# The last 64 contraction rows of a Q projection as pairs of 64-row tiles in front of the transpositions, with the order of all steps and the PSUM banks in a table

## The chip, the cores and the metric

The kernel runs on one core of one Trainium2 chip. The metric is the device time of one execution in microseconds. A core has five engines that work side by side: PE (matmuls, on an array of 128 by 128), DVE and ACT (elementwise work and reductions), POOL, and SP, which here issues most DMAs. Each engine runs its own list of instructions in order and waits on semaphores for the others. PE's results go to PSUM, which has 8 banks of 512 f32 values per partition; DVE and ACT bring them to SBUF.

## The reference

Two independent attention problems, A and B, of the same size, whose outputs are put side by side. Each projects x to queries, attends with 32 query heads over 16 cached key and value heads, and projects the result:

```python
B, Sq, D = 16, 80, 576
Hq, Hkv, Sk, Dh = 32, 16, 512, 128
q = (x @ wq).reshape(B, Sq, Hq, Dh).transpose(0, 2, 1, 3)
k = jnp.repeat(k_cache, 2, axis=1)
v = jnp.repeat(v_cache, 2, axis=1)
scores = jnp.einsum("bhqd,bhkd->bhqk", q, k) * Dh ** -0.5
p = softmax(scores, axis=-1)
o = jnp.einsum("bhqk,bhkd->bhqd", p, v)
out = o.transpose(0, 2, 1, 3).reshape(B, Sq, Hq * Dh) @ wo
```

All inputs are bf16. The Q projection contracts over D = 576 = 4 x 128 + 64 rows.

## The kernel before

**Units.** The work is cut into 128 units, numbered U: one batch entry and four key/value heads, so eight query heads of 80 rows each. Eight units (eight batch entries) of the same heads form an octet, `goct`; there are 16 octets, 8 per problem.

**Steps of a unit.** Scores stand with the query rows on the partitions. The two query heads of one key head have 160 rows: 128 of them form one whole-array matmul of 512 columns (`qk`, L686, four per unit), and the last 32 rows of all four key heads form one more score tile from four matmuls of 32 columns of the array (`qkr`, L672). For each of the five score tiles DVE takes the maximum (`max`, L695), ACT the exponential with its row sum (`exp`, L699), DVE the reciprocal of the sums (`rcp`, L705) and POOL the normalised rows (`nrm`, L708). Then 40 transpositions, `tr` (L741), bring the probabilities to key rows on the partitions. They are issued in 20 pairs: one half of a pair uses array rows 0 to 63, the other rows 64 to 127 (`tile_position=(64 * h, 0)`), and the two write different PSUM banks. Three copies (`ptev`, L758 on ACT, L760 on DVE) bring them to `pT`. The `pv` matmuls (L778: four groups per unit, four matmuls of 160 columns each) multiply with V; ACT copies two groups at a time into `oT` (`oev`, L794).

**Q projection.** For each octet, `em_qp` (L568) computes `qT` for the eight heads in two parts of the octet's 640 rows, 480 and 160 columns. Every part is five matmuls of 128 rows that add up in one bank. The fifth holds the 64 rows left over: `xT[:, half, 4]` holds the last 128 columns of x transposed, so its first 64 rows repeat rows that chunk 3 has, and the first 64 rows of `wq_sb[:, :, 4]` are zero (`em_wqz`, L400). ACT or DVE scales and stores the result (`qev`, L579 and L580).

**Output projection.** `op` (L828) multiplies 16 heads of `oT` by `wo` in tiles of 128 rows and 288 columns. The first half of the heads is copied to `acc` (L841, L843); the second is added to it (L859) and stored.

**Loads.** SP issues K as a transposing DMA (L640, five slots `kT`), V (L644, four slots), the weights, x and the stores. A K load waits until the last `qk` of the unit five earlier has read its slot. Problem A's x is transposed on PE (L492), problem B's by two DMAs per half (`em_ldxt` L509, `em_ldxt4` L513).

**Order.** Every step is added to `_Sched` with a key, resources that it reads and writes, and estimates of its duration. `arrange` plans with these: at each point it takes for the engine that is free first the ready step with the lowest priority value, picks one of the PSUM banks that the step's class may use (`BANKS`), and, on PE, groups steps of the same tile shape (`mode`: 0 whole array, 1 for `qkr`, 2 for `tr`). `finalize` derives the semaphore waits from the order that comes out, and each engine issues its own steps in that order. `LA` = 10 is how many score tiles the scores run ahead, `QL0`, `QL1` and `QL2` how many units ahead Q is done. One semaphore more, `e_tr`, makes the transposition group wait in its own middle.

Of the kernel before, what the change touches and what calls it, by code (L numbers as in the profile page):

```python
# [6 lines left out]
BF16 = mybir.dt.bfloat16  # L7
# [6 lines left out]
LA = 10  # L14
# [5 lines left out]
NS = 16  # L20
QL0 = 14.0
QL1 = 10.0
KC = 2.95
VK = 8.0
KK = 8.0
DLAT = 1.6
XC = 0.4
QL2 = 10.0
VC = 1.65
WQC = 3.2  # L30
NQ = 3
# [6 lines left out]
BANKS = dict(S=(0, 1, 2), T=(3, 4, 6), Y=(4, 6, 5), O=(5, 7, 4), M=(7, 5, 6, 3, 4), M0=(7, 5, 6, 3, 4), M1=(7, 6, 5), ML=(7, 5, 6, 0, 1))  # L38
NML = 12
XDMA = True  # L40
RG = ((0, 1, 2), (3, 4))
TS0 = 4.5
TSAME = 0.3
TNEXT = 0.05
# [5 lines left out]
PTO = -2.0  # L50
PTE = (('dve',), ('dve',), ('act', 'dve'))
QEV = ('act', 'dve')
OEO = 3.0
OVO = 2
QEO = 0.0
RCO = 3
NSS = 6
OPSPLIT = 2
XLD = ((-100.0, -60.0), (-25.0, -24.9))
XH = -2.0  # L60
WQ1 = -16.8
OPX = ((12.0, 1.8), (18.5, 1.45), (18.5, 1.45), (18.5, 1.45))
LP0 = 19
LPS = 1.05
LPC = 29.0
WOL = 1.2
WOA = (99.0, 99.0, 99.0, 99.0)
WOS = 1.0

MM0 = 0.0025  # L70
MM1 = 1.0 / 2400.0


def _mm(n, cols):
    return n * (cols * MM1 + MM0)


class _VB:
    __slots__ = ("cls", "phys", "left", "id")

    def __init__(self, cls, i):
        self.cls = cls
        self.phys = None
        self.left = 0
        self.id = i


class _Op:
    __slots__ = ("engs", "eng", "key", "seq", "emit", "reads", "writes", "dsem", "stream", "dur", "lat", "cost",
                 "alloc", "pri", "after", "pre", "start", "done", "mode",  # L90
# [3 lines left out]
class _Sched:  # L94

    def __init__(self):
        self.ops = []
        self.marks = {}
        self.nvb = 0

    def bank(self, cls):
        self.nvb += 1
        return _VB(cls, self.nvb)

    def add(self, eng, key, emit, reads=(), writes=(), dsem=None, name="", stream=None, dur=0.1, lat=0.15,
            cost=0.0, alloc=(), mode=0, ahead=0.0, after=None):
        op = _Op()
        op.engs = (eng,) if isinstance(eng, str) else tuple(eng)
        op.eng = op.engs[0]
        op.key = float(key)  # L110
        op.pri = op.key - ahead
        op.after = after
# [7 lines left out]
        op.dur = dur  # L120
        op.lat = lat
        op.cost = cost
        op.alloc = list(alloc)
        op.mode = mode
        op.deps = []
        op.pre = []
        op.start = op.done = None
        op.signals = False
        op.sidx = None
        op.waits = []  # L130
        op.clock = None
        self.ops.append(op)
        return op

    def arrange(self):
        ops = sorted(self.ops, key=lambda o: (o.key, o.seq))
        last_w, readers = {}, {}
        for op in ops:
            deps = {}
            for r, ver in op.reads:  # L140
                if isinstance(r, _VB):
                    r.left += 1
                w = last_w.get(r)
                assert w is not None, ("read of never-written resource", r, op.name)
                deps[id(w)] = w
            for r, ver in op.writes:
                w = last_w.get(r)
                if w is not None:
                    deps[id(w)] = w
                for rd in readers.get(r, ()):  # L150
                    deps[id(rd)] = rd
            deps.pop(id(op), None)
            for r, ver in op.reads:
                readers.setdefault(r, []).append(op)
            for r, ver in op.writes:
                last_w[r] = op
                readers[r] = []
            op.pre = list(deps.values())
        streams = {}
        for op in ops:  # L160
            streams.setdefault(op.stream, []).append(op)
        by_eng = {}
        for name, l in streams.items():
            assert all(o.engs == l[0].engs for o in l), name
            for e in l[0].engs:
                by_eng.setdefault(e, []).append(name)
        at = dict((name, 0) for name in streams)
        free = dict((e, 0.9) for e in by_eng)
        mode = 0
        bank_free = dict((b, 0.0) for b in range(8))  # L170
        dma_free = 1.4
        left = len(ops)
        hold = dict(pe=0.05, dve=0.02, act=0.02, pool=0.0, sp=0.0)

        def pick(vbs, now, used=()):
            if not vbs:
                return []
            c = sorted((max(bank_free[b], now), n_, b) for n_, b in enumerate(BANKS[vbs[0].cls])
                       if bank_free[b] is not None and b not in used)
            for t, n_, b in c:  # L180
                r = pick(vbs[1:], now, used + (b,))
                if r is not None:
                    return [(t, b)] + r
            return None

        def ready(o, now):
            t = 0.0
            if o.after is not None:
                d = self.marks[o.after]
                if d.start is None:  # L190
                    return None
                t = d.start
            for d in o.pre:
                if d.done is None:
                    return None
                if not (d.eng == "pe" and o.engs[0] == "pe"):
                    t = max(t, d.done)
            if o.alloc:
                c = pick(o.alloc, max(t, now))
                if c is None:  # L200
                    return None
                t = max([t] + [bank_free[b] for _, b in c])
            return t

        while left:
            best = None
            for e in free:
                cand = []
                for n in by_eng[e]:
                    if at[n] < len(streams[n]):  # L210
                        o = streams[n][at[n]]
                        r = ready(o, free[e])
                        if r is not None:
                            cand.append((r, o))
                if cand:
                    st = max(free[e], min(c[0] for c in cand))
                    if best is None or st < best[0]:
                        best = (st, e, cand)
            assert best is not None, [(streams[n][at[n]].name, [d.name for d in streams[n][at[n]].pre if d.done is None],
                                       len(streams[n][at[n]].alloc)) for n in streams if at[n] < len(streams[n])]  # L220
            now, e, cand = best
            if e == "pe":
                near = [c for c in cand if mode and c[1].mode and c[0] <= now + (TSAME if c[1].mode == mode else TNEXT)]
                cand = [c for c in near if c[1].mode == mode] or near or cand
                now = max(now, min(c[0] for c in cand))
            k_, s_, r, o = min(((o.pri, o.seq, r, o) for r, o in cand if r <= now + hold[e]), key=lambda x: x[:2])
            st = max(now, r)
            o.eng = e
            dur = o.dur[e] if isinstance(o.dur, dict) else o.dur
            if e == "pe":  # L230
                if o.mode and mode == 0 or o.mode != mode:
                    st = max(st, now + 0.1)
                mode = o.mode
            if o.alloc:
                for vb, (_, b) in zip(o.alloc, pick(o.alloc, max(r, now))):
                    vb.phys = b
                    bank_free[b] = None
            o.start = st
            free[e] = st + dur
            if o.dsem is not None:  # L240
                d0 = max(st + 0.5, dma_free)
                dma_free = d0 + o.cost
                o.done = dma_free + DLAT
            else:
                o.done = st + dur + o.lat
            for res, ver in o.reads:
                if isinstance(res, _VB):
                    res.left -= 1
                    if res.left == 0:
                        bank_free[res.phys] = o.done  # L250
            at[o.stream] += 1
            left -= 1
        self.end = max(o.done for o in ops)
        for n_, op in enumerate(sorted(ops, key=lambda o: (o.start, o.seq))):
            op.key = float(n_)
# [72 lines left out]
def bass_concat_heads__gqa_block_cached__gqa_block_cached__near_ridge_kernel(  # L328
# [27 lines left out]
    with ExitStack() as es:  # L356
# [42 lines left out]
        def em_wqz(e):  # L399
            return e.memset(wq_sb[0:64, :, 4, :], 0.0)  # L400
# [544 lines left out]
```

## Time and profile before

| | us |
|---|---|
| median of 3 runs | 739.16 (739.05 to 739.34) |
| the profiled execution | 739.38 |
| its span in the profile | 737.6 |
| PE, DVE, ACT, POOL busy in it | 730.7, 650.3, 625.7, 433.8 |
| granted TensorE clock, mean | 1.0 |

The largest PE groups by busy time are L568 (Q projection, 1280 matmuls, 206.0 us), L778 (PV, 2048, 189.4), L686 (scores, 512, 185.7), L828 (output projection, 1280, 180.5), L741 (transpositions, 5120, 96.9) and L672 (remainder scores, 512, 39.6).

How to read it: a group's busy time and mean duration come from records whose ends are modelled for PE, and matmuls are pipelined, so a matmul's record (233 ns for 160 columns) is longer than the distance from its start to the next matmul's start. Sums of PE's work are made from these distances. "us to landing" of a DMA is from its issue to the semaphore. Idle time is given with what released it.

### The profile page before, as it was taken

What the parts mean: (1) busy time and instruction counts of PE and PEld (TensorE: products, weight loads), DVE (VectorE), ACT (ScalarE), POOL (GpSimd) and SP (SyncE); (2) the same over time, 40 slices, a digit from 0 to 9 for tenths busy, and PEclk for the clock granted to TensorE, in tenths of its full rate; (3) what the DMA queues carried; (4) which work ended last, traced back from release to release, by engine and by line L of the source; (5) the groups of instructions that cost most, each with busy time, mean ns of one, the idle gap of its engine ahead of it and who ended that gap; (6) DMA issues with size and microseconds to landing.
All of it is one profiled execution on the core that took longest, in us unless ns stands there. A gap on an engine that the chain in (4) does not pass through costs nothing.

```text
span 737.6 us, 26159 instructions
## 1 busy us (share of the span) xinstructions
PE 730.7 (99%) x10818; PEld 510.8 (69%) x10818; DVE 650.3 (88%) x1344; ACT 625.7 (85%) x1827; POOL 433.8 (59%) x647
## 2 busy tenths in 40 slices
PE   9999999999999999999999999999999999999998
PEld 5566677677667676677677677666777677667776
DVE  4989999998999999888999999998889888998983
ACT  1889999999989889878889888989899888898881
POOL 1465666665666576556666565575565565665660
DMA  9999999999999999999999889999988978999920
GB/s 263 217 281 229 262 227 252 227 223 211 200 224 213 210 237 268 228 239 226 213 234 228 196 185 275 261 273 228 198 188 192 203 169 173 295 235 217 198 94 29
DMA packets 362102, 160.85 MB, mean 218 GB/s; under 512 B 276096, under 2 KB 358528, under 8 KB 361984
## 3 DMA queue, kind: packets, MB, share of 16 engines
q1 hardware_dynamic: 360768, 158.00, 97.3%
q8 instruction: 85, 1.39, 0.8%
q10 hardware_dynamic: 1216, 1.18, 0.5%
q14 instruction: 33, 0.27, 0.1%
HBM read 87.46 MB, written 2.95 MB: 123 GB/s over the span
## 4 chain that ended last, share of the span: by engine, by line
PE 96%; DVE 2%; ACT 1%; ACTq 0%; issue 0%
PE ps L568 23%; PE ps L828 21%; PE ps L778 19%; PE ps L686 15%; PE ps L741 12%; PE ps L672 5%; DVE negmax L695 1%; ACT p_sb L699 1%; PE ps L492 0%; DVE qT L580 0%; PE ps L429 0%; ACTq L545 0%; ACT oT L794 0%; ACT L448 0%; DVE pT L760 0%
## 5 line engine op out<-in xcount | busy, mean ns | idle before, releaser
L708 POOL TENSOR_SCALAR p_sb<-p_sb,rinv 128x512 bf16<-128x512 bf16 x640 | 431.4, 692 | 285.4 <-DVE rinv L705 283.5
L699 ACT ACTIVATE p_sb<-ps,negmax 128x512 bf16<-128x512 f32 x640 | 443.1, 701 | 27.8 <-DVE negmax L695 24.2
L695 DVE TENSOR_REDUCE negmax<-ps 128x1 f32<-128x512 f32 x640 | 416.2, 679 | 32.6 <-PE ps L672 16.8
L568 PE MATMUL ps<-xT,wq_sb 128*128 128x160 bf16 (+1 forms) x1280 | 206.0, 300 | 1.0 <-DVE xT L496 0.6
L778 PE MATMUL ps<-pT,v_sb 128*128 128x160 bf16 x2048 | 189.4, 233 | 0.0
L686 PE MATMUL ps<-kT,qT 128*128 128x512 bf16 x512 | 185.7, 380 | 0.0
L828 PE MATMUL ps<-wo_sb,oT 128*128 128x288 bf16 x1280 | 180.5, 286 | 0.0
L778 PEld LDWEIGHTS ps<-pT,v_sb 128*128 128x128 bf16 x2048 | 155.0, 98 | 35.1 <-DVE pT L760 0.6
L760 DVE COPY pT<-ps 128x1024 bf16<-128x1024 bf16 (+1 forms) x260 | 172.1, 676 | 6.0 <-PE ps L741 5.1
L568 PEld LDWEIGHTS ps<-xT,wq_sb 128*128 128x128 bf16 x1280 | 106.5, 98 | 66.1 <-issue 1.7
L828 PEld LDWEIGHTS ps<-wo_sb,oT 128*128 128x128 bf16 x1280 | 122.5, 98 | 40.6 <-issue 2.1
L699 ACT ACTIVATION_READ_ACCUMULATOR p_sb<-ps,negmax 128x1 f32 x640 | 137.5, 215 | 0.0
L794 ACT CAST oT<-ps 128x320 bf16<-128x320 f32 x256 | 108.7, 430 | 15.0 <-PE ps L778 14.1
L741 PEld LDWEIGHTS ps<-ident,p_sb 64*128 64x128 bf16 x5120 | 81.8, 95 | 37.9 <-issue 9.9
L741 PE MATMUL ps<-ident,p_sb 64*128 64x64 bf16 x5120 | 96.9, 190 | 0.0
L580 DVE TENSOR_SCALAR qT<-ps 128x480 bf16<-128x480 f32 (+1 forms) x131 | 65.2, 500 | 15.6 <-PE ps L568 14.7
L758 ACT COPY pT<-ps 128x256 f32<-128x256 f32 x124 | 47.3, 381 | 36.0 <-PE ps L741 35.4
L579 ACT ACTIVATE qT<-ps 128x160 bf16<-128x160 f32 (+1 forms) x125 | 52.8, 443 | 15.0 <-PE ps L568 14.3
L686 PEld LDWEIGHTS ps<-kT,qT 128*128 128x128 bf16 x512 | 49.6, 98 | 21.7 <-ACT p_sb L699 2.4
L705 DVE RECIPROCAL rinv<-rowsum 128x3 f32<-128x3 f32 (+1 forms) x256 | 41.2, 161 | 8.2 <-ACT p_sb L699 7.8
L672 PE MATMUL ps<-kT,qT 128*32 128x512 bf16 x512 | 39.6, 384 | 1.6 <-ACT p_sb L699 1.6
L859 DVE TENSOR_TENSOR osb<-ps,acc 128x288 bf16<-128x288 f32 x40 | 18.0, 451 | 16.1 <-PE ps L828 15.5
(25 smaller groups left out, 48.6 us busy)
## 6 DMA issues: line engine op xcount, KB each, us to landing
v_sb<-in_A_v_cache_dram SPq DMA_DIRECT2D x64, 512.0 KB, 4.8
v_sb<-in_B_v_cache_dram SPq DMA_DIRECT2D x64, 512.0 KB, 4.6
wo_sb<-in_A_wo_dram SPq DMA_DIRECT2D x8, 576.0 KB, 6.9
wo_sb<-in_B_wo_dram SPq DMA_DIRECT2D x8, 576.0 KB, 6.2
wq_sb<-in_B_wq_dram SPq DMA_DIRECT2D x4, 1024.0 KB, 7.1
out_dram<-osb SPq DMA_DIRECT2D x40, 72.0 KB, 3.7
wq_sb<-in_A_wq_dram SPq DMA_DIRECT2D x2, 1024.0 KB, 6.7
wq_sb<-in_A_wq_dram ACTq DMA_DIRECT2D x2, 512.0 KB, 6.9
```

The lines of the kernel that those rows point to most:

```text
L568: last = e.matmul(ps[:, vb.phys, 0:n1 - n0], lhsT=wq_sb[:, wsl, ck, i * 128:(i + 1) * 128], rhs=xT[:, half, ck, n0:n1], start=(ck == 0), s ...
L580: return e.tensor_scalar(dst, src, SCALE, None, op0=AluOpType.mult)
L672: last = e.matmul(ps[32 * g4:32 * g4 + 32, vb_.phys, :], lhsT=qT[:, qsl_, bl_, g4 * 160 + 128:g4 * 160 + 160], rhs=kT[:, ks_, :, g4 * 128: ...
L686: return e.matmul(ps[:, vb.phys, :], lhsT=qT[:, qsl, bl, gl * 160:gl * 160 + 128], rhs=kT[:, ks, :, gl * 128:(gl + 1) * 128], start=True, ...
L695: return e.tensor_reduce(negmax[:, si:si + 1], ps[:, vb.phys, :], axis=AX.X, op=AluOpType.max, negate=True)
L699: return e.activation(p_sb[:, psl, :], ps[:, vb.phys, :], AF.Exp, bias=negmax[:, si:si + 1], scale=1.0, accum_out=rowsum[:, ss, k:k + 1])
L708: return e.tensor_scalar(p_sb[:, psl, :], p_sb[:, psl, :], rinv[:, ss, k:k + 1], 1.0, op0=AluOpType.mult, op1=AluOpType.mult)
L741: last = e.matmul(dst, lhsT=p_sb[64 * h:64 * h + 64, psls[k_], j * 128:(j + 1) * 128], rhs=ident[64 * h:64 * h + 64, 64 * h:64 * h + 64], ...
L760: return e.tensor_copy(dst, src.rearrange("p (n c) -> p n c", n=16))
L778: last = e.matmul(ps[:, vo.phys, off:off + 160], lhsT=v_sb[:, vs, gl, j * 128:(j + 1) * 128], rhs=pT[:, pts, 4 * gl + j, :], start=(j == 0 ...
L794: return e.copy(dst, src)
L828: last = e.matmul(ps[:, vb.phys, 0:DC], lhsT=oT[:, hi, rb * 128:(rb + 1) * 128], rhs=wo_sb[:, wi, c3 * DC:(c3 + 1) * DC], start=(hi == 0), ...
```

## The change

The 64 rows left over in the Q projection are no longer padded to 128. Chunk 4 of `xT` now holds the last 64 columns of x twice, on partitions 0 to 63 and again on 64 to 127; a new tile `wt` holds the last 64 rows of `wq` for two pairs of heads on the lower and for the other two pairs on the upper partitions.

Q is now done in pieces of two batch entries (160 columns) and four heads: eight pieces `m` per octet, each with two banks `vbq`, one for two heads. `em_qp` does the 4 x 128 rows: 8 matmuls per bank, 16 per piece. `em_qt` does the tail: four matmuls of 64 rows and 160 columns, issued alternately on array rows 0 to 63 into the first bank and on rows 64 to 127 into the second. From unit 2 on a piece belongs to a unit (`us = u0 - LQ + m`, LQ = 11), and its tail is issued inside `em_tr` of that unit, right in front of the 20 pairs of transpositions; the transpositions' first four pairs, of the remainder tile, go into the free columns of the same two banks. The 13 pieces due earlier have their tails as steps of their own. Two evictions of 320 columns per piece (`qev`) take the place of one of 480 and one of 160 per head; the remainder's copy to `pT` becomes two (`prev`), so a unit has four copies there instead of three.

For problem A, POOL copies the last 64 columns of x beside themselves (`em_xrp`) and PE transposes the pair (`em_xtt`); for problem B the two copies come by two plain loads (`em_ldxs`) and PE transposes them (`em_xtr2`), where before a second transposing DMA brought chunk 4.

`arrange` no longer plans. A table, `ORDER`, names for each step in turn the stream whose next step comes; a quote mark moves an eviction from DVE to ACT, and digits give its PSUM banks. `e_tr`, the clearing of `wq_sb` and the steps on `wtest` and `wfac` are gone; `acc` copies and `oT` copies may now be on DVE or ACT. `NQ` falls from 3 to 2 buffers of `qT`, and `LA` becomes 11.

In the built programs PE has 2048 whole-array and 512 tail matmuls for Q, where it had 640 of 480 and 640 of 160 columns, and 60 transpositions of x where it had 50. DVE has 90 wide and 133 narrow `pT` copies, 137 `qev`, 130 `oev` and 23 `acc` copies (before: 256 and 4, 131, none and none); ACT has 166 and 123, 119, 126 and 17 (before: none and 124, 125, 256 and 40).

The core of the diff:

```diff
     def arrange(self):
...
+        table = iter("".join(ORDER.split()))
+        n = 0
+        for c in table:
+            other = c == "'"
+            op = next(lines[next(table) if other else c])
+            if op.alt:
+                op.eng = op.alt[other]
+            for vb in op.alloc:
+                vb.phys = int(next(table))
+            op.key = float(n)
+            n += 1
...
-                    def em_qp(e, i=i, wsl=wsl, half=half, n0=n0, n1=n1, vb=vb):
-                        last = None
-                        for ck in range(5):
-                            last = e.matmul(ps[:, vb.phys, 0:n1 - n0],
-                                            lhsT=wq_sb[:, wsl, ck, i * 128:(i + 1) * 128],
-                                            rhs=xT[:, half, ck, n0:n1], start=(ck == 0), stop=(ck == 4))
-                        return last
+                    def em_qp(e, h=h, hq=hq, wsl=wsl, half=half, n0=n0, vbq=vbq):
+                        last = None
+                        for r in range(2):
+                            hi = 4 * hq + 2 * h + r
+                            for ck in range(4):
+                                last = e.matmul(ps[:, vbq[h].phys, QO + 160 * r:QO + 160 * r + 160],
+                                                lhsT=wq_sb[:, wsl, ck, hi * 128:(hi + 1) * 128],
+                                                rhs=xT[:, half, ck, n0:n0 + 160], start=(r == 0 and ck == 0), stop=False)
+                        return last
...
+                def em_qt(e, hq=hq, wsl=wsl, half=half, n0=n0, vbq=vbq):
+                    last = None
+                    for r in range(2):
+                        for h in range(2):
+                            last = e.matmul(ps[:, vbq[h].phys, QO + 160 * r:QO + 160 * r + 160],
+                                            lhsT=wt[64 * h:64 * h + 64, wsl, hq, r * 128:(r + 1) * 128],
+                                            rhs=xT[64 * h:64 * h + 64, half, 4, n0:n0 + 160],
+                                            start=False, stop=(r == 1), tile_position=(64 * h, 0))
+                    return last
...
-            def em_tr(e, psls=tuple(psls), vbs=(vx, vz), vy=vy, U=U):
+            def em_tr(e, psls=tuple(psls), vtq=vtq, vtp=vtp, td=td):
                 last = None
+                if td:
+                    td["emit"](e)
                 for n_ in range(20):
-                    if n_ == 16:
-                        e.wait_ge(sems["e_tr"], U + 1)
+                    k_, j = divmod(n_, 4)
                     for h in range(2):
-                        k_, j = divmod(n_, 4)
-                        k_ = (k_ + 1 - h) % 5
                         if k_:
                             c_ = ((k_ - 1) * 4 + j) * 64
-                            dst = psb[:, vbs[h].phys, c_:c_ + 64]
+                            dst = psb[:, vtp[h].phys, c_:c_ + 64]
                         else:
-                            dst = psb[:, vy.phys, 0:512].rearrange("p (g j c) -> p g j c", g=4, j=4)
-                            dst = dst[:, 2 * h:2 * h + 2, j, :]
+                            dst = psb[:, vtq[h].phys, 0:256].rearrange("p (g j c) -> p g j c", g=2, j=4)[:, :, j, :]
```

More of the change, by code (lines that the diff above doesn't have):

```diff
@@ L13 @@
 GR = 2
-LA = 10
+LA = 11
 NK = 5
@@ L88 @@
 class _Op:
[L89 to L90 removed]
+    __slots__ = ("eng", "key", "seq", "emit", "reads", "writes", "dsem", "stream", "alloc", "alt",
                  "deps", "signals", "sidx", "waits", "clock", "name")
@@ L135, in arrange @@
     def arrange(self):
[L136 to L158, printed above, removed]
@@ L171, in arrange @@
[L171 to L184, printed above, removed]
@@ L186, in ready @@
[L186 to L252, printed above, removed]
@@ L504, in bass_concat_heads__gqa_block_cached__gqa_block_cached__near_ridge_kernel @@
+                S.add("dve", xk + 2.5, em_xte, reads=[R(vb, 0)], writes=[R(("xt", half, k_), 0) for k_ in range(k0, k1)],
+                      name="xe%d.%d" % (half, part), stream="xe2")
         for half in range(NPP):
```

496 lines of the change are left out of this document (276 added, 220 removed).

## The prediction, made before the changed kernel ran

> **What bounds the kernel now.** I read the busy shares first, then the chain of work that ended last, then PE's waits.
>
> ```profile
> PE 730.7 (99%) x10818; PEld 510.8 (69%) x10818; DVE 650.3 (88%) x1344; ACT 625.7 (85%) x1827; POOL 433.8 (59%) x647
> ...
> PE 96%; DVE 2%; ACT 1%; ACTq 0%; issue 0%
> ```
>
> PE ends almost every step of the chain. As its ends are modelled, "99%" alone would prove little; the waits, and the distance from one matmul's start to the next, decide.
>
> ```profile
> PE ps L672 <- ACT p_sb L699: 1.6, 1, 1.6
> PE ps L414 <- DVE ps L439: 1.2, 1, 1.2
> PE ps L568 <- DVE xT L496: 0.6, 1, 0.6
> PE ps L568 <- ACT qT L579: 0.4, 1, 0.4
> PE ps L492 <- ACT wtest L448: 0.3, 1, 0.3
> PE ps L492 <- DVE xT L496: 0.2, 1, 0.2
> ```
>
> After its first matmul PE waits 3.1 us in all (these rows without the 1.2). PE's work is the time, so a step on PE is worth its spacing of starts. The timeline shows those:
>
> ```profile
> 299.64 0.99 PE L778 MATMUL ps<-pT,v_sb 128*128 128x160 bf16 x12
> 300.47 0.38 PE L686 MATMUL ps<-kT,qT 128*128 128x512 bf16 x1
> 300.79 0.76 PE L741 MATMUL ps<-ident,p_sb 64*128 64x64 bf16 x40
> 301.48 0.39 PE L686 MATMUL ps<-kT,qT 128*128 128x512 bf16 x1
> 301.70 0.51 PE L568 MATMUL ps<-xT,wq_sb 128*128 128x160 bf16 x5
> 302.05 0.38 PE L686 MATMUL ps<-kT,qT 128*128 128x512 bf16 x1
> 302.26 1.19 PE L568 MATMUL ps<-xT,wq_sb 128*128 128x480 bf16 x5
> ```
>
> Twelve L778 take 0.83 us from first start to next start: 69 ns for 160 columns, each with new weights. Over all records of a kind: 69.4 ns for 160 columns, 202.8 for 480, 216 for 512, 122.6 for 288. L686 to L741 is 0.32 us where L686 to L568 is 0.22: going from whole-array matmuls to 64-row tiles costs 0.096 us, and coming back as much (0.122 instead of 0.026 after the last transposition). The 40 transpositions (20 pairs) hold 0.69 us with that: 29 ns a pair, where 64 columns at the 480-column rate plus the fixed part come to the same 29. So the two of a pair cost as one.
>
> **Part by part.**
>
> *Main Q matmuls.* Before: 640 x 202.8 + 640 x 69.4 = 174.2 us. After: 2048 of 160 columns and 128 rows, 142.1 us. Nearest row: L778, same shape and new weights each time, or L568's own 160-column rows.
>
> *Tails.* 512 matmuls of 64 rows and 160 columns, 256 pairs. Paired as transpositions are: 256 x 69.4 = 17.8 us; one after the other: 35.5. I take 17.8: same tile shape, same array halves, two banks, as L741. Q falls by 174.2 - 142.1 - 17.8 = 14.3 us.
>
> *Tile changes.* In the built orders PE changes tile shape 333 times before, 352 after (13 tails stand alone, so do more transpositions): 19 x 0.096 = +1.8 us. From tail to transposition only the transposing flag changes; whole-array L429 to L492 shows no charge for that (0.22 and 0.06 us, bare column times). Bound: 115 x 0.096 = +11.0; I take 0.
>
> *x transpositions.* 60 of 128 columns instead of 50, 56 ns each: +0.6 us. Two DMA transpositions of B's x become four plain loads.
>
> PE's sum: -14.3 + 1.8 + 0.6 = **-11.9 us**.
>
> A rule against this: L568's weight loads take 98 ns each by the groups, longer than 69 ns of columns, yet starts stay 69 ns apart, so the loads are hidden. The Trainium skill ("TensorE: Matmul & The Clock Gate", Back-to-back issue gap) has load and matmul together set the pace, about 81 ns at 128 columns. By that figure as an estimate the 1408 added 160-column matmuls would cost some 16.3 us more; this trace disagrees, with 69.4 ns.
>
> *Evictions.* Start to start, when queued, DVE takes 0.60 us for a max (L695) or a 1024-wide pT copy (L760), about 0.08 less than the record. For Q it is 0.575 at 480 columns and 0.231 at 160, hence 0.40 at 320; a 256-wide copy, from 1024 and 512 (0.33), 0.20. ACT: exp with its read 0.67; Q 0.45 and 0.18, hence 0.32; a 1024-wide pT copy, from 256 f32 at 0.25 and Q's 0.83 ns a column, 0.46.
>
> ```profile
> L760 DVE COPY pT<-ps 128x1024 bf16<-128x1024 bf16 x256 | 170.8, 680 | 6.0 <-PE ps L741 5.1
> L580 DVE TENSOR_SCALAR qT<-ps 128x480 bf16<-128x480 f32 x72 | 47.0, 653 | 15.0 <-PE ps L568 14.2
> L580 DVE TENSOR_SCALAR qT<-ps 128x160 bf16<-128x160 f32 x59 | 18.3, 312 | 0.6 <-PE ps L568 0.5
> ```
>
> With the built counts DVE goes from 631 to 619 us (640 maxes 383; pT 54 + 26; Q 55; oT 52; the rest 49), ACT from 586 to 604 (exps 428; pT 77 + 18; Q 38; oT 38; acc 5). Both stay under PE's 712, so the mean hides them. Two stretches of the written order do not. Between the maxes of scores 605 and 625 (units 118 to 122) DVE has 23 maxes, 7 + 3 pT copies, 4 oT copies, 10 reciprocals and one sum, 21.3 us, and ACT 20.5; PE has 17 + 4 score matmul times, 6 transposition groups, 23 PV groups and 14 tile changes, 15.9. Excess 5.4 us: neither Q nor output work stands there. Around units 4 to 9 DVE has 25.4 us against 22.9, excess 2.5. Before, the largest excess is 3.3 us, in the first units, and PE's waits there are 0.6 + 0.4 + 0.2, so some 2.1 us is absorbed by banks in hand. After: 3.3 + 0.4 = 3.7 us of waits (0 to 7.9).
>
> *K loads.* PE's one long wait is put down to an exp that was long done; a K load with a 7.12 us issue landed 0.3 us before that matmul:
>
> ```profile
> 295.12 7.12 SPq L640 DMA_TRANSPOSE kT<-in_A_k_cache_dram  x1
> ...
> DMA to landing us min/median/max: 4.1/6.1/11.7
> ```
>
> PE's work between the last use of a K slot and its next use is 14.8 us or more before; after, 9.3, 9.7, 10.0 and 10.4 us at units 63, 101, 59 and 65. The median landing fits, the longest does not: 0 to 7.4 us, and I take 2, as three of the four lie among B's first loads, where the wait of before was. SP has six more small Q-side loads (ldwt and xst for ldwb and ldxtb), 0.5 us each; its waits for slots hide them, else +3 us on SP, seen only by K.
>
> *Transposition to PV.* The tightest distance on PE falls from 1.85 to 1.08 us, with a tenth of the units under 1.85, and two copies per half must fit in: 0.6 to 0.9 us if the engine is free, up to one max (0.6) later if not. 0 to 7 us; I take 1. The Q evictions now wait for the whole transposition group, but Q is 11 units ahead.
>
> *Added and lost waits on PE.* A transposition group now also waits for wt and xT's tail; everything on PE stands behind it, but those land units earlier. The removed wait on e_tr, the clearing of wq_sb (POOL) and the wtest steps: nothing, no PE wait names them but the 0.3 at L492. At the start PE's second step now waits for a copy on POOL behind the x load: 0 to +0.5, within the above.
>
> Waits after: 3.7 + 2 + 1 = 6.7, before 3.1: +3.6. The profiled execution took 739.38 us (span 737.6), 0.2 above the median of 739.16. 739.4 - 11.9 + 3.6 = 731.1; I say **731.0**.
>
> **The rivals.**
>
> *The tails do not pair.* Price +17.8 us: 748.8. For it: no row shows two 64-row tiles adding 160 f32 columns into two banks; L741 writes bf16. Against: L741 pairs fully, and the four 32-column tiles of L672 run 512 f32 columns in the time of one. The place is the four tail matmuls ahead of a transposition: 0.14 us if paired, 0.28 if not; the change turns slower when over 8.3 of the 17.8 us of overlap, about half, is lost. 7%.
>
> *The engines that empty PSUM, or K, become the bound.* The two stretches, K and PV cost their upper parts: 10 to 14 us of waits, hence 735 to 739.5. For it: the excesses are in the order as built. Against: DVE's whole work is 93 us less than PE's. 15%. The Trainium skill ("TensorEngine Tiling (Array Packing)", PSUM Bottleneck) says that tiling speeds TensorE and not the emptying of PSUM; here Q's evicted columns stay equal.
>
> *No new waits.* The order hides all, and before's go: 723.5 to 727.5. For it: before hides DVE at 87% of PE's work. 14%.
>
> *Weight loads set the pace.* If 98 ns spaced the added 1408 matmuls, +40 us: 771. Against it stand all 160-column rows. 2%; the page cited above says something of this kind.
>
> **How the numbers follow.** My forecast (727.5 to 735) has 62%. About 0.2% is what a measurement of this kernel tells from no change: 737.7 to 740.6. Faster: 62 + 14 + 10 of the 15 = 86%; same 3%; slower 7 + 2 + 2 = 11%. Range: below 725.5 lies half of the no-new-waits case (7%), above 738.0 some 13%: 725.5 to 738.0.
>
> **What would show it.** Q's main matmuls 69 ns apart, 2048 of them; the first transposition 0.14 us after the first tail of its group; 0.096 us at tile changes; PE waits of about 7 us, half between 660 and 705 us ended by maxes or exps, the next largest before score matmuls around units 59 to 65; DVE and ACT busy about as long as before. I am wrong if the tails take 0.28 us, if PE's steady spacings change, or if its waits pass 12 us.

## The result, and the profile after

| | us (median, lowest to highest, runs) | ratio to before, 95% interval |
|---|---|---|
| before, measured again | 738.88 (737.65 to 741.42, 18) | 1 |
| after | 747.36 (739.43 to 752.69, 18) | 1.0104 [1.0084, 1.0123] |

The change made the kernel 1.0% slower; 731.0 was forecast, and 738.0 was the upper end of the range. The ratio leaves out the two longest runs after, 751.83 and 752.69 us, which count as a slower state. The profiled execution took 748.76 us, its span is 747.0. First the busy shares and the shares of the chain of after:

```profile
PE 727.6 (97%) x12108; PEld 566.7 (76%) x12108; DVE 639.3 (86%) x1468; ACT 640.0 (86%) x1832; POOL 433.9 (58%) x650
...
PE 81%; DMA 8%; ACT 8%; SPq 2%; DVE 1%; issue 1%; ACTq 0%
```

PE had 96% of the chain before and has 81% now. DMA and SP's queue, absent before, hold 10%. PE's waits, in the same view as before (us in total, times, longest):

```profile
PE ps L756 <- DMA v_sb<-in_A_v_cache_dram: 3.9, 3, 2.2
PE ps L646 <- DMA kT<-in_A_k_cache_dram: 2.4, 3, 1.8
PE ps L713 <- ACT oT L770: 1.5, 2, 0.9
...
PE ps L756 <- ACT p_sb L672: 0.8, 1, 0.8
PE ps L659 <- ACT p_sb L672: 0.7, 3, 0.3
PE ps L713 <- ACT p_sb L672: 0.7, 1, 0.7
```

PV (L756) now waits for V, the remainder's scores (L646) for K. V was in no row before. Some of these rows name an engine that had long been done: the 0.8 us put down to L672 ends 0.13 us after V0 landed. So I took each wait from the starts in the trace, as the distance to the step before less its bare time, and gave it to the dependency that ended last, loads by their landing:

| PE's time, us | before | after | forecast |
|---|---|---|---|
| Q on the whole array | 174.3 | 142.5 | -32.1 |
| tails | | 19.1 | +17.8 |
| tile changes, 333 and 352 at 0.096 | 32.0 | 33.8 | +1.8 |
| x transpositions | 3.1 | 3.9 | +0.6 |
| PV groups | 142.0 | 143.7 | 0 |
| the two warm-up groups | 4.9 | 6.3 | 0 |
| waits on V | 0 | 6.4 | 0 |
| waits on K | 1.6 | 3.8 | 2, before's 1.6 gone |
| waits on exps and evictions | 2.0 | 5.9 | 4.7 |
| other waits (start, wo, under 0.12 each) | 1.4 | 4.9 | |
| scores, transpositions, output | 372.2 | 372.3 | 0 |
| end of the last matmul | 734.9 | 744.2 | -8.3 |

The rows add up to the last line but for the 1.2 us before PE's first matmul and some tenths. PE's waits grew by 16 us. The rest of its time fell by 6.9: the first four rows by 10.1, while PV and the warm-up, for which nothing was forecast, took 3.1 back. The matmuls themselves did nearly what was forecast. One unit in the timeline of after:

```profile
311.27 1.27 PE L528 MATMUL ps<-xT,wq_sb 128*128 128x160 bf16 x16
...
312.38 0.38 PE L659 MATMUL ps<-kT,qT 128*128 128x512 bf16 x1
...
313.57 0.38 PE L659 MATMUL ps<-kT,qT 128*128 128x512 bf16 x1
313.88 0.31 PE L543 MATMUL ps<-xT,wt 64*128 64x160 bf16 x4
314.03 0.75 PE L713 MATMUL ps<-ident,p_sb 64*128 64x64 bf16 x40
314.71 0.60 PE L659 MATMUL ps<-kT,qT 128*128 128x512 bf16 x2
```

Sixteen L528 take 1.11 us, 69.4 ns each. L659 to L543 is 0.31 us, the 0.216 of 512 columns and 0.096 for the tile change. From the first tail to the first transposition it is 0.15 us: the tails pair.

The rows of the evictions, which answer to L760 and L580 of before:

```profile
L726 DVE COPY pT<-ps 128x1024 bf16<-128x1024 bf16 x90 | 60.8, 682 | 8.7 <-PE ps L713 7.8 <-PE ps L756 0.4
L557 DVE TENSOR_SCALAR qT<-ps 128x320 bf16<-128x320 f32 x137 | 64.7, 479 | 5.4 <-ACT pT L731 3.7 <-PE ps L543 1.3
```

DVE is busy 11 us less than before, ACT 14 us more, near the forecast. Now SP's queue around the longest wait on V, in the timeline of after:

```profile
63.35 4.67 SPq L614 DMA_TRANSPOSE kT<-in_A_k_cache_dram  x1
68.06 0.58 SPq L618 DMA_DIRECT2D v_sb<-in_A_v_cache_dram  x1
68.68 5.08 SPq L614 DMA_TRANSPOSE kT<-in_A_k_cache_dram  x1
73.81 1.12 SPq L584 DMA_DIRECT2D wo_sb<-in_A_wo_dram  x2
74.98 0.51 SPq L618 DMA_DIRECT2D v_sb<-in_A_v_cache_dram  x1
...
82.68 0.69 PE L756 MATMUL ps<-pT,v_sb 128*128 128x160 bf16 x4 [2.16 <-DMA v_sb<-in_A_v_cache_dram]
```

V9's slot was free at 64.2 us. Its load stood in SP's list behind a transposing K load, which held the queue for 5.08 us, and two loads of wo; it was issued at 74.98 and landed at 82.54. PE stood until 82.68.

That wait cost more than its 2.2 us. Behind it the array ran at half its clock for 3.4 us, as the column PEclk shows (1.00 is the full clock):

```profile
core 0: us, PE busy (x) PEld busy (x) DVE busy (x) ACT busy (x) POOL busy (x), PEclk, DMA share, GB/s
82.30:85.80 3.50, 3.12 (x22) 2.87 (x23) 1.09 (x2) 1.83 (x6) 0.95 (x2) 0.51 1.26 232
```

The distances between starts double there, to 133 ns for 160 columns and 427 for 512, and PE loses another 1.5 us. Most of it stands in the table in the rows of PV (0.7) and Q (0.5).

Over all V loads, the median from a free slot to the issue was 2.3 us before and is 5.4 now; the margin from landing to use that 5% of them fall below was 5.3 us before and is 0.1 now.

### The profile page after: what moved, and what is told of

The parts are those of the page before. It is cut to its first block, busy times and chain, and to the rows that moved or that the text cites. A ratio compares the mean times of both kernels' runs of the same rounds, so it can differ in the third digit from the quotient of the medians.

```text
span 747.0 us, 28953 instructions
## 1 busy us (share of the span) xinstructions
PE 727.6 (97%) x12108; PEld 566.7 (76%) x12108; DVE 639.3 (86%) x1468; ACT 640.0 (86%) x1832; POOL 433.9 (58%) x650
## 4 chain that ended last, share of the span: by engine, by line
PE 81%; DMA 8%; ACT 8%; SPq 2%; DVE 1%; issue 1%; ACTq 0%
PE ps L805 20%; PE ps L756 16%; PE ps L528 16%; PE ps L659 13%; PE ps L713 8%; ACT p_sb L672 5%; DMA kT<-in_A_k_cache_dram 5%; PE ps L646 4%; PE ps L543 3%; DMA v_sb<-in_A_v_cache_dram 2%; SPq L614 2%; ACT pT L724 1%; DVE negmax L668 1%; ACT oT L770 1%; DMA wo_sb<-in_A_wo_dram 1%
## 5 line engine op out<-in xcount | busy, mean ns | idle before, releaser
L672 ACT ACTIVATE p_sb<-ps,negmax 128x512 bf16<-128x512 f32 x640 | 447.4, 719 | 42.2 <-DVE negmax L668 38.5
L756 PE MATMUL ps<-pT,v_sb 128*128 128x160 bf16 x2048 | 194.9, 233 | 6.4 <-DMA v_sb<-in_A_v_cache_dram 3.9
L756 PEld LDWEIGHTS ps<-pT,v_sb 128*128 128x128 bf16 x2048 | 152.8, 98 | 42.8 <-ACT p_sb L672 8.0
L659 PE MATMUL ps<-kT,qT 128*128 128x512 bf16 x512 | 177.6, 381 | 1.2 <-ACT p_sb L672 0.7
L528 PE MATMUL ps<-xT,wq_sb 128*128 128x160 bf16 x2048 | 178.7, 233 | 0.0
L528 PEld LDWEIGHTS ps<-xT,wq_sb 128*128 128x128 bf16 x2048 | 150.1, 98 | 21.7 <-ACT p_sb L672 1.5
L672 ACT ACTIVATION_READ_ACCUMULATOR p_sb<-ps,negmax 128x1 f32 x640 | 149.0, 233 | 0.0
L724 ACT COPY pT<-ps 128x512 f32<-128x512 f32 x166 | 98.9, 613 | 13.9 <-PE ps L713 13.5
L770 ACT CAST oT<-ps 128x320 bf16<-128x320 f32 x126 | 56.6, 456 | 18.9 <-PE ps L756 18.5
L557 DVE TENSOR_SCALAR qT<-ps 128x320 bf16<-128x320 f32 x137 | 64.7, 479 | 5.4 <-ACT pT L731 3.7
L770 DVE CAST oT<-ps 128x320 bf16<-128x320 f32 x130 | 62.1, 479 | 8.2 <-PE ps L756 7.4
L726 DVE COPY pT<-ps 128x1024 bf16<-128x1024 bf16 x90 | 60.8, 682 | 8.7 <-PE ps L713 7.8
L556 ACT ACTIVATE qT<-ps 128x320 bf16<-128x320 f32 x119 | 53.7, 462 | 12.6 <-PE ps L543 10.7
L659 PEld LDWEIGHTS ps<-kT,qT 128*128 128x128 bf16 x512 | 47.8, 97 | 22.0 <-ACT p_sb L672 3.9
L733 DVE COPY pT<-ps 128x256 bf16<-128x256 bf16 x133 | 36.2, 281 | 12.9 <-PE ps L713 11.7
L646 PE MATMUL ps<-kT,qT 128*32 128x512 bf16 x512 | 39.4, 384 | 2.9 <-DMA kT<-in_A_k_cache_dram 2.4
```

The lines of the kernel that those rows point to most:

```text
L528: last = e.matmul(ps[:, vbq[h].phys, QO + 160 * r:QO + 160 * r + 160], lhsT=wq_sb[:, wsl, ck, hi * 128:(hi + 1) * 128], rhs=xT[:, half, ck ...
L557: return e.tensor_scalar(dst, src, SCALE, None, op0=AluOpType.mult)
L646: last = e.matmul(ps[32 * g4:32 * g4 + 32, vb_.phys, :], lhsT=qT[:, qsl_, bl_, g4 * 160 + 128:g4 * 160 + 160], rhs=kT[:, ks_, :, g4 * 128: ...
L659: return e.matmul(ps[:, vb.phys, :], lhsT=qT[:, qsl, bl, gl * 160:gl * 160 + 128], rhs=kT[:, ks, :, gl * 128:(gl + 1) * 128], start=True, ...
L672: return e.activation(p_sb[:, psl, :], ps[:, vb.phys, :], AF.Exp, bias=negmax[:, si:si + 1], scale=1.0, accum_out=rowsum[:, ss, k:k + 1])
L724: return e.copy(pT[:, pts, :, :].bitcast(F32)[:, :, 32 * h:32 * h + 32], ps[:, vtp[h].phys, :].rearrange("p (n c) -> p n c", n=16))
```

## The experiments

My theory after the result: the loads are late because of where they stand in SP's list, so that a shorter or better ordered list mends it; the pairing is not at fault. Rivals: too few slots; too much traffic; the tails. Every kernel below is the changed one with the edit shown, except b_noKV, which is the kernel before.

**K and V loads cut to a corner** (V, K, both, and both in the kernel before). The edit for V is shown; K's is the same, and puts a plain load in the place of the transposing one:

```diff
             def em_ldv(e, ...):
+                if U >= NV:
+                    return e.dma_start(v_sb[:, vs, 0, 0:64], vc_ap[b, 4 * q, 0:128, 0:64])
```

a_noV: 

> The changed kernel, with V loaded in full for units 0 to 3 only; later V loads keep their place, semaphore and waits but move 16 KB instead of 512 KB (the output is then not attention's). In the profile of the changed kernel PE waits 18.3 us (waits over 0.12 us): 6.4 end with a V load, 3.8 with a K load, 0.3 with wo, the rest with DVE, ACT and the start. Theory 'loads': SP's queue of loads, which runs without a pause from 0 to 100 and from 250 to 350 us, sets the pace there, so the saved PE time became waits. Then the V waits go and most K waits with them, since K has the DMA engines alone: 747 falls to 737 to 740. Rival 'order': the written order of evictions and banks sets the time, and a load that comes earlier is followed by a wait for a max or an exp: 744 to 747.

a_noK: 

> The changed kernel, with K loaded in full for units 0 to 4 only; later K loads are plain copies of 16 KB at the same place (output not attention's). K's issue takes 3 to 4.5 us of SP's queue each, so by 'loads' SP is then idle most of the time and both V and K waits go: 736 to 740. By 'order' 744 to 747. If a_noV brings the V waits down and this one does not bring down more than the 3.8 us of K, then V's own transfer and not its place behind K was late.

a_noKV: 

> The changed kernel with both K and V as 16 KB copies after the first 5 and 4 units (output not attention's). Its PE waits are then those of evictions and of the start. 'Loads': 748.8 of the profiled execution minus 10.4 us of load waits, 736 to 739, and the runs lie as close together as those of before (within 0.3%) where the changed kernel spreads over 739 to 753. 'Order': 744 to 747. The waits between 690 and 707 us (4.0 us, ended by maxes, exps and copies) stay in both.

b_noKV: 

> The kernel before with the same 16 KB copies for K and V (output not attention's): what it waits for loads. It has one such wait of 1.6 us, so by both theories 736 to 738. Against a_noKV this gives what the tails and the order are worth without loads: PE's own work fell by some 10 us by the starts of its matmuls, so if a_noKV is not well below b_noKV, waits for evictions hold the rest.

| | us | ratio to before | waits over 0.12 us |
|---|---|---|---|
| a_noV | 737.23 (736.04 to 738.61) | 0.998 [0.9967, 0.9993] | 11.5 |
| a_noK | 735.37 (734.70 to 736.54) | 0.9954 [0.994, 0.9968] | 9.5 |
| a_noKV | 735.47 (734.69 to 737.14) | 0.9956 [0.9943, 0.9968] | 7.9 |
| b_noKV | 737.85 (737.45 to 738.36) | 0.9986 [0.9974, 0.9997] | 2.9 |

By the ratios the K and V loads, with all that hangs on them, cost the changed kernel 11 us and the kernel before 1. They are not two costs that add: either kind taken out gives back 9 to 11, as is to be expected when both stand in one list. Without these loads the change gains 2.4 us, not the 8.3 forecast: the last matmul ends 2.8 us earlier (733.0 to 730.2), with waits 5.0 us higher, so the rest of PE's time falls by 7.8. It would have fallen by 1.7 more if the second warm-up of a_noKV had run at full speed, as that of b_noKV did (see the last section).

**The order of SP's list.** a_edf keeps every step of the other engines and sorts SP's steps, within the same places, by the step that needs them (`due`: the first step that reads what is loaded, for K and x 20 places earlier; `rel`: the last step that holds the slot):

```diff
+        for k_ in slots:                     # SP's places in the table
+            o = min((o for o in todo if rel[id(o)] < k_), key=lambda o: (due[id(o)], o.seq))
+            todo.remove(o)
+            o.key = k_
```

> The changed kernel, all work and all bytes the same; only the order of the loads in SP's list differs: at each place of SP's list stands the load that is needed first among those whose slot is free by then (K counted 20 steps of the table earlier than it is needed). In the changed kernel the V loads were issued 5.4 us (median) after their slot was free, behind K loads that hold SP for 3 to 4.5 us each. Theory 'place': the loads are late because the table puts them there; the waits for loads fall from 10.4 us to 4 or less, and the time to 738 to 742. Rival 'rate': SP and the DMA engines cannot bring the loads sooner in the first 150 and from 250 to 400 us, whatever their order: 745 to 749.

739.75 us (737.93 to 742.25), ratio 1.0013 [0.9998, 1.0028]: by the ratios 6.7 us of the 7.7 lost are back, with the same loads, slots and bytes. PE's waits in a_edf:

```profile
PE ps L561 <- DMA wq_sb<-in_A_wq_dram: 2.0, 1, 2.0
PE ps L746 <- issue: 1.9, 1, 1.9
PE ps L746 <- ACT oT L803: 1.4, 2, 0.9
PE ps L381 <- DVE wo_sb L374: 1.2, 1, 1.2
```

No row names K or V; the load left over is the first Q weights at 12 us. So the place in the list was the cause of most of the loss. Two more pieces of time in this run are not a matter of the list alone. Behind the wait on the Q weights the array is again at half its clock, which costs another 1.5 us (columns as above):

```profile
12.90:16.40 3.50, 3.50 (x26) 2.31 (x27) 1.06 (x3) 0.87 (x3) 0.00 (x0) 0.51 1.16 215
```

And the second row, "issue" (a wait with no releaser in the trace), stands inside a group of 40 transpositions, where the kernel waits for nothing:

```profile
39.18 0.69 PE L746 MATMUL ps<-ident,p_sb 64*128 64x64 bf16 x35
41.77 0.24 PE L746 MATMUL ps<-ident,p_sb 64*128 64x64 bf16 x5 [1.91 <-issue]
```

**More slots** (a_slots):

```diff
-NK = 5
-NV = 4
+NK = 6
+NV = 5
```

> The changed kernel with 6 slots for K instead of 5 and 5 for V instead of 4, the same table. If loads are late because a slot comes free late ('slots'), the waits for loads fall to 4 us or less: 738 to 742. By 'place' and by 'rate' the list of SP is what they wait for, not the slot: 744 to 748.

743.45 us (743.38 to 743.88), ratio 1.006 [1.0037, 1.0083]. The time lies between the ranges of the two theories. Waits on K and V fell from 10.2 to 6.9 us, but the longest, on V9 behind the K load in SP's list, stayed:

```profile
PE ps L756 <- DMA v_sb<-in_A_v_cache_dram: 2.0, 1, 2.0
```

I read this as: a slot more helps where the slot held a load up, and not where the list did.

**V from another queue** (a_Vpool):

```diff
-            S.add("sp", 5.0 * U - VK, em_ldv, ...
+            S.add("pool", 5.0 * U - VK, em_ldv, ...
```

> The changed kernel with the V loads issued by POOL, at the same place of the table, instead of SP: K and V no longer stand behind each other. POOL is busy 434 of 747 us. 'Place': V waits (6.4 us) go and K waits shrink, 739 to 743, unless POOL's list, which waits for normalisation steps in order, makes V later. 'Rate' (the 16 DMA engines are shared): 745 to 749.

825.71 us (816.46 to 845.75), 11 to 15% slower, at a granted clock of 0.969 in the profiled run. V's loads in it:

```profile
L618 POOL DMA_DIRECT2D v_sb<-in_A_v_cache_dram x64: 748/797/941, 20.3 to 412.0; - x64
...
DMA to landing us min/median/max: 4.3/5.7/21.5
```

A V load holds POOL 0.80 us (min/median/max in ns), where SP gave 0.58, and lands up to 21.5 us later. The longest rows of PE's waits are these:

```profile
PE ps L713 <- issue: 20.0, 5, 6.8
PE ps L756 <- issue: 9.3, 5, 3.8
PE ps L528 <- issue: 7.8, 2, 7.5
```

All twelve stand inside groups of matmuls, where the kernel waits for nothing. They make 37 us of the 72 that PE's rows of waits add up to (16 in after), and the clock not granted is another 25 (0.031 of 817.9 us). So most of what this run lost came from neither the slots nor SP's list. It speaks against moving V to POOL, and decides nothing on the theory. The Trainium skill ("DMA: Bandwidth & Descriptors", Issuing engines are not separate DMA queues) says that several issuing engines save only issue time; here even that was not saved.

**The tails on the whole array** (a_full in the table's order, a_edf_full in a_edf's):

```diff
-   lhsT=wt[64 * h:64 * h + 64, ...], rhs=xT[64 * h:64 * h + 64, half, 4, ...], tile_position=(64 * h, 0)
+   lhsT=wt[:, ...], rhs=xT[:, half, 4, ...]
```

a_full: 

> The changed kernel with the four tail matmuls as four whole-array matmuls one after the other, in the same place and the same order of everything else (they add both halves' products, so Q is not the projection). One part undone: PE's work grows by 4 x 69.4 - 150 = 0.13 us per tail, 16 us in all, less some tile changes. If PE sets the pace throughout, 747 becomes 762 to 764. If loads and evictions set it in stretches, part of the 16 us fills waits that are there anyway: 753 to 759. Either way above the 747 of the changed kernel: the pairing itself is a gain.

a_edf_full: 

> The queue order of a_edf, and the tails as four matmuls on the whole array, over both heads' rows, in place of pairs of 64-row tiles (the Q of this kernel adds the other head's rows, so its outputs differ). Four times 69 ns in place of 151 ns for 128 tails is 16 us of TensorE more. Theory, that pairing is worth its whole 16 us once no load is late: 739.75 plus 12 to 16, so 752 to 755.5, since only the waits on evictions (about 5 us) can hide any of it. Rival, that the 8.7 us measured in the order of the table is all that pairing is worth: 748.5.

756.05 us (755.52 to 756.75), ratio 1.023 [1.0206, 1.0254], and 756.15 (754.70 to 756.83), ratio 1.0226 [1.0208, 1.0244]. By the ratios unpaired tails cost 15.7 us over a_edf, but only 9.3 over the changed kernel: there the longer PE time let the loads land, and their waits fell from 10.2 to 4.7 us. Pairing is worth some 16 us; in the table's order some 6 us of what it saved on PE came back as waits.

**The stretch near the end.** Busy time of each engine in 15 us around the transpositions of units 119 to 121, in after:

```profile
692.00:707.00 15.00, 12.21 (x247) 8.30 (x248) 14.80 (x34) 15.00 (x48) 13.02 (x20) 1.00 1.07 259
```

In the same window of before PE is busy for the whole 15 us, DVE for 13.3 and ACT for 13.4. In after DVE and ACT are full and PE waits 4.0 us; 3.3 was forecast. a_edf_end moves two output projection tiles, 3.9 us of PE, from 666 to 680 us into this stretch, and gives eight steps there other banks:

```diff
+        at = {"op1.1.0.8.0": 5019.1, "op1.1.0.8.1": 5019.2, "oeb1.0.8": 5022.5, "st1.0.8": 5022.6,
+              "op1.1.0.9.0": 5092.1, "op1.1.0.9.1": 5092.2, "oeb1.0.9": 5096.2, "st1.0.9": 5096.3}
...
+            op.key = at.get(op.name, op.key)
```

> The queue order of a_edf, and the last two output projection tiles of the earlier half (four groups of eight 288-column matmuls, 3.9 us of TensorE) taken from 666 to 680 us and put ahead of the transpositions of units 119 and 121, with their VectorE sums, where TensorE waits 4.0 us between 682 and 697 us for exponentials and evictions. Theory, that the evictions there fall behind only because nothing else is left for TensorE: those waits fall below 1 us, some new ones appear where the tiles stood, and the time falls from 739.75 to 736.5 (736 to 738). Rival, that VectorE and ScalarE set the pace from 664 us on, so that the waits only move forward: 739 to 740, with 3 to 4 us of waits between 664 and 690 us.

741.79 us (739.46 to 747.19), ratio 1.0039 [1.0022, 1.0055], slower than a_edf by the two ratios and above the 739 to 740 of the rival too. In the waits the rival holds: they moved forward. PE's waits between 664 and 700 us in a_edf_end:

```profile
PE ps L754 <- ACT p_sb L713: 1.0, 1, 1.0
PE ps L700 <- ACT p_sb L713: 0.9, 3, 0.4
PE ps L700 <- ACT qT L597: 0.8, 1, 0.8
PE ps L754 <- ACT oT L811: 0.4, 1, 0.4
```

By starts, waits over 0.12 us are 3.9 us between 667 and 684, where a_edf has 0.4, and 2.2 from there on, where it has 3.6. The engines that empty PSUM were already close to their pace where the tiles were taken away.

**The start** (a_edf_es, on top of a_edf_end: the loads of `wt` for octet 0 after the second load of `wq_sb` in ACT's queue):

```diff
-                        S.add(eng, t_ld + 0.001 * r + 0.001, ...
+                        S.add(eng, t_ld + (0.001 if goct else 15.0) + 0.001 * r, ...
```

> As a_edf_end, and the two loads of the last 64 rows of the first Q weights stand behind the first instead of ahead of the second load of the main rows in ScalarE's queue. In a_edf TensorE waits 2.18 us at 12 us for that second load, issued at 2.70 and landed at 12.04 us, behind K0's transposing load. Theory, that the order of issue sets this: it is issued at 1.3 us, lands before 9, and the time falls by another 1.5 to 2.2 us, to 734.5. Rival, that K0's load, which lands at 14.1 us, holds the start anyway: within 0.5 us of a_edf_end, the wait of 2.2 us then standing in front of the first score matmul.

740.51 us (739.23 to 741.94), ratio 1.0017 [1.0004, 1.0029], so 1.3 less than a_edf_end, a little under the 1.5 to 2.2 expected. The wait of 2.2 us at 12 us is gone; three of 0.3 to 0.8 us, on the first weights and K0, stand in its place between 10.9 and 13.0 us. PE reaches unit 7 3.1 us earlier than in a_edf, not all by this edit: the half clock behind that wait (1.5 us) is gone too, and the stall in the transpositions at 38 us is 1.7 us shorter. V10, issued at 85.0 us behind K14 and K15, then made PE wait 2.3 us.

**All of it by order** (a_new: the table of steps rewritten with a_edf's list, a_edf_es's start, four loads moved in SP's list, and the order, banks and eviction engines from unit 106 on). Of SP's list:

```diff
- ldk2 ldk3 ldwa1.0 ldx1.0 ldwt1.0 ldwt1.1 ldx1.1
+ ldk2 ldwa1.0 ldx1.0 ldwt1.0 ldwt1.1 ldk3 ldx1.1
...
- ldwo0.0.0 ldwo0.0.1 ldwo0.0.2 ldwo0.0.3 ldk14 ldk15 ldv10
+ ldwo0.0.0 ldwo0.0.1 ldv10 ldwo0.0.2 ldwo0.0.3 ldk14 ldk15
```

> The queue order of a_edf with three more edits, all in the order of work alone. (1) Start: the second load of the first Q weights ahead of their last 64 rows, as in a_edf_es. (2) SyncE's list: the second pair's Q weights and the half-1 x rows ahead of K3 (which waits 6 us for its use in a_edf_es), and V10 between the wo loads, ahead of K14 and K15 (in a_edf_es it is issued behind them at 85.0 us and lands 2.27 us late). (3) From unit 106 on a new order and new PSUM banks, found by replaying the last 120 us of a_edf with its own measured durations: output projection tiles 7, 8 and 9 of the earlier half stand in units 117, 119 and 121, and 75 evictions change between VectorE and ScalarE. Theory, that what a_edf still loses against its own TensorE work are waits that order sets: the end gives 3.2 us by the replay, the start 1.6 (a_edf_end to a_edf_es, with V10's 2.3 us still in it) plus 2.3 for V10 and 0.5 for the Q weights, so 739.75 - 7.6 = 732.2, at worst 735 if half of it turns up elsewhere: faster than the kernel before by 0.5 to 0.9%. Rival, as a_edf_end showed, that waits only move: 738 to 741.

737.22 us (734.72 to 740.31), ratio 0.9972 [0.9953, 0.999]: faster than before by 0.3%, and than the change as made by 1.3%, by the two ratios. The gain is less than the 732.2 to 735 expected. Between 664 and 700 us only four rows are left:

```profile
PE ps L713 <- ACT oT L770: 0.2, 1, 0.2
PE ps L713 <- DVE oT L770: 0.2, 1, 0.2
PE ps L543 <- issue: 0.2, 1, 0.2
PE ps L756 <- ACT p_sb L672: 0.2, 1, 0.2
```

By starts, waits over 0.12 us there are 1.7 us, 4.0 in a_edf: 2.3 of the 3.2 expected came. The start was 3.1 us ahead of a_edf at 70 us and 1.2 at 525: 1.1 went into the first wo matmul (0.7) and a K load (0.4) at 84 to 87 us, where V10 had waited, and 1.2 went into two stalls inside groups (0.7 in transpositions at 365 us, 0.5 in PV at 432), against one wait of 0.6 that a_edf alone has at 311. Here three edits are measured together.

## Why the prediction was wrong, step by step

**The failing step is "Waits after: 3.7 + 2 + 1 = 6.7".** It came to 21.0 us by starts, which passes the 12 us that the prediction itself gave as proof against it. By terms:

- *Evictions, 3.7.* Right in place and size for the last stretch: 4.0 us for 3.3. The early stretch gave 1.0 for 0.4.
- *K loads, 2.* 3.8 us. The largest, 1.9 us, is at unit 63, which was named; others are at units 51 and 57, not among B's first loads, and none at 101. (The load behind before's one long wait landed at 306.47 us, 0.1 and not 0.3 before the matmul.)
- *V loads.* No term at all. They cost 6.4 us: 2.2 at unit 9, 1.7 at 44, 1.0 at 0, 0.8 at 2. The prediction measured the distance between the uses of a K slot and not of a V slot, whose smallest on PE fell from 15.9 to 8.6 us by the same count.
- *Transposition to PV, 1.* Right in size: of PV's waits over 0.12 us that no V load ended, two are in front of a group, 0.8 us together.
- *The measure itself.* Slot distance was held against the time from issue to landing. A load also waits for its issue. With the 5.2 us of landing in the table of V loads below and the median 5.4 us from free slot to issue, V needs 10.6 us, more than 8.6.

```profile
L618 SPq DMA_DIRECT2D v_sb<-in_A_v_cache_dram x64: 367/576/1499, 25.1 to 388.6; - x64
...
DMA to landing us min/median/max: 3.9/5.2/8.8
```

The prediction had a row for this in hand: a K load with a 7.12 us issue. It used it for that load's own landing, and not for the load behind it. Nor did it place the loads: it says of SP's added loads that waits for slots hide them, but in after SP's issues follow one another without a pause from 1 to 119 us and from 238 to 332. So they did in before, from 1 to 160 and from 257 to 401: SP was as busy there, and the loads had more time in hand (5.3 us for 0.1, above). All of the waits on V and K lie before 394 us.

**PE's sum, -11.9.** Measured -6.9 in the profiled run of after. At full clock and without stalls the sum comes to -32.1 + 19.1 + 1.8 + 0.6 = -10.6, so only the tails were mis-sized; clock and stalls took most of the rest.

- *Main Q matmuls*: 142.5 for 142.1, the rest in the stretch at half clock. *Tile changes* and *x transpositions*: near the forecast, +1.8 and +0.8.
- *Tails*: they pair, and the 115 changes from tail to transposition show no charge. Four take 149 ns in the mean, where two pairs of 69.4 would take 139: the starts are 3 ns apart within a pair, and 76 ns lie between the last of the first pair and the second pair. +1.3 us for the term.
- *PV groups*, +1.7 us, were not in the sum: 0.7 is the half clock behind the wait on V9, 0.8 two stalls inside groups at 258 and 442 us.
- *Second warm-up*, +1.4 us, below.

**The rivals.** "The tails do not pair" is false: a_edf_full shows what that would cost. "Weight loads set the pace" is false: 2048 matmuls 69.4 ns apart. The page that it names, "TensorE: Matmul & The Clock Gate" of the Trainium skill, gives some 81 ns at 128 columns; the trace disagrees on the changed kernel too. "No new waits" is false by the 16 us. "The engines that empty PSUM, or K, become the bound" came nearest in kind, but it had no V, and stopped at 739.5. A rival "a load queue becomes the bound" was missing.

**Signs.** Spacing of Q, the 0.096 us and the first transposition after the first tail (0.15 for 0.14): right. Waits of 7 us, half between 660 and 705: the half near the end was there, the rest came to 17 us, five times its forecast. DVE and ACT: right.

**What stays open.** The profiled runs of a_edf and a_noKV differ by 4.5 us. In a_edf the wait on the first Q weights is 2.2, the half clock behind it 1.5 and the stall inside the transpositions 2.1; its second warm-up, at full clock, gives 1.7 back. Whether such stalls go with the order or with the traffic was not tried. The after kernel's own times spread over 13 us, before's over 4. With loads that land at a margin of 0.1 us a little more or less DMA time would do that; a_edf's spread is 4 us again, and a_noKV's 2.5. The clock may have a part in it: its granted mean in the 18 runs after is 1.0 in four, 0.998 in eleven and 0.995 in three, and 0.002 of it is 1.5 us. No run was made to show the spread in one wait.

## What to carry to other kernels

When PE's work shrinks, list every stream of loads with slots, and hold the shrunken distance between uses of a slot against the wait for issue plus issue plus landing, not the landing alone. Where one queue carries short loads and transposing ones, its order is part of the change: sort it by the step that needs each load before giving out slots or queues. A step taken off the bounding engine brings its price only as far as the next engine's pace allows: in one order pairing was worth 9 us, in another 16. And a wait of 2 us on the bounding engine can cost 1.5 us more by the clock behind it.

## What the runs showed of the hardware

- The issue of a K load, a transposing DMA, holds SP's queue for 3.1 to 3.9 us in the median and up to 8.0; the issue of a plain load of the same 512 KB, 0.58:

```profile
L614 SPq DMA_TRANSPOSE kT<-in_A_k_cache_dram x64: 1791/3875/7956, 1.8 to 348.3; - x64
L614 SPq DMA_TRANSPOSE kT<-in_B_k_cache_dram x64: 1302/3121/7378, 353.4 to 705.8; - x64
```

- The second warm-up, the same eight matmuls, in after and then in a_edf:

```profile
L363 PE MATMUL ps<-wo_sb 128*128 128x512 bf16 x8 | 3.6, 631 | 0.5 <-DVE wo_sb L352 0.5
```

```profile
L396 PE MATMUL ps<-wo_sb 128*128 128x512 bf16 x8 | 1.9, 380 | 0.5 <-DVE wo_sb L385 0.5
```

Mean 631 ns in one run and 380 in another, the steps before them being the same. The Trainium skill ("TensorE: Matmul & The Clock Gate", Part 1: The HAM clock gate) has a free-running window of about 3.4 us decide when the array goes from half to full clock; the two durations agree with that, and a start is thus worth 1.7 us more or less by chance (3.6 us for 1.9).
- The array can fall to half its clock behind a wait of PE of some 2 us, for 3.4 us: from 82.3 us in after and from 12.9 in a_edf. It need not: behind the wait of 2.3 us in a_edf_es the granted clock is 1.00. What decides between the two is not shown.
- The stalls inside groups look like PE waiting for its own instructions. In the traces a 16 KB packet of queue 8, of the kind "instruction", ends 1.2 to 1.7 us before the end of each of the twelve in a_Vpool, of five in after and of the one in a_edf. No run was made to test it.
- Paired tiles of 64 rows that add up f32 in two banks run together like those that transpose bf16: 3 ns apart.
